# Issuing all large stores of the backward part from GpSimd, in a decode attention block with its gradients

## Chip, cores, metric

One core of one Trainium2 chip. The metric is the device time of one launch in microseconds (us), the median of several runs; lower is better.

## The reference

A pre-norm decode block, forward and backward (the vector-Jacobian product of the whole), for 4 batches and one query position. Cut to what matters:

```python
def _A_ref(x, k_cache, v_cache, wq, wo):            # B=4, H=32, Sk=4096, Dh=128, D=512
    q = (x @ wq).reshape(B, 1, H, Dh).transpose(0, 2, 1, 3)
    p = softmax(einsum("bhqd,bhkd->bhqk", q, k_cache) * Dh ** -0.5)
    o = einsum("bhqk,bhkd->bhqd", p, v_cache)
    return o.transpose(0, 2, 1, 3).reshape(B, 1, H * Dh) @ wo
h   = x + _A_ref(layernorm(x), ...)
out = h + (silu(layernorm(h) @ w1) * (layernorm(h) @ w3)) @ w2
# returned: out and the gradients of x, k_cache, v_cache, wq, wo, w1, w3, w2
```

What counts is the traffic. K and V have 128 (batch, head) pairs of 1 MB each in bf16. The forward part reads K and V once. The backward part reads V again and writes two gradients of the same size, gk (of the K cache) and gv (of the V cache): 128 x 3 MB, and some 20 MB of weights and weight gradients. Each gk and gv is an outer product of a column and a row, so they are cheap to make and dear to write.

## The kernel before

All big tiles live in 22 slots of 8 KB per partition, handed out from a queue: what is given back goes to its end, what is taken comes from its front. The rotation is fixed when the program is built; a slot whose last user is a store is waited for until that store has landed.

```python
free = deque(range(NSLOT))                 # NSLOT = 22
class Slot:
    def __init__(self, name):
        self.i = free.popleft()
        self.t = slotp.tile([P, SLOT], BF16, name=name, tag=f"slot{self.i}")
    ...
    def give(self):
        free.append(self.i)
```

The backward loop. `front` transposes V on TensorE (ScalarE copies the result out) and makes dP; `back` makes gv and gk on VectorE and stores them. GpSimd copies a column of P ahead of each gv. Loads of V run up to 7 heads ahead.

```python
def load_V2():
    ...
    nc.sync.dma_start(out=V2s[s].heads(), in_=cache_head(A_v_cache, s))        # L749
def front(s):
    ...                                                     # transposes of V, dP on TensorE
    nc.gpsimd.tensor_copy(out=P2[:], in_=P_all[:, s, :, None].to_broadcast([P, SJ, 2]))
def back(s):
    gv = Slot("gv")
    outer(gv.heads(), P2, reps["rdo", s // REP][:, s % REP, :])                # VectorE
    nc.gpsimd.dma_start(out=rows_of(out_3[b, h]), in_=gv.heads())              # L1065
    gv.give()
    ...                                                     # dS from dP, c, P
    gk = Slot("gk")
    outer(gk.heads(), dS2, reps["rq", s // REP][:, s % REP, :])                # VectorE
    nc.sync.dma_start(out=rows_of(out_2[b, h]), in_=gk.heads())                # L1075
    gk.give()
for s in range(NH):
    prefetch(s + 1)                                         # load_V2 while slots allow
    if s + 1 < NH: front(s + 1)
    back(s)
    step("s", 1 if s < 42 else 2 + s % 2)                   # a piece of the weight gradients
```

The weight gradients (gwq, gw of w2, w1 and w3, gwo) are made beside this by `side_work`, in 14 tiles, for example:

```python
for h0 in range(0, H, 8):
    st = Slot("gwo")
    for k in range(8):
        h = h0 + k
        grad_unit(st.b(8 * D)[:, k * D:(k + 1) * D], oflat.b(HD)[0:B, h * P:(h + 1) * P], dh_bf[0:B, :])
        yield
    nc.sync.dma_start(out=out_5[h0 * P:(h0 + 8) * P, :].rearrange("(h p) j -> p h j", p=P), ...)   # 1 KB rows in HBM
    st.give()
```

## Time and profile before

| | before |
|---|---|
| median, 3 runs | 1774.19 us (1772.02 to 1779.35) |
| profiled run | 1788.03 us, 0.8% above that median |
| backward part | 735 us to the end, DMA share 0.99, 396 GB/s |
| DMA queues there | q1 (SyncE) 278.63 MB, q0 (GpSimd) 134.23 MB |

In the slices of a page every digit is a tenth of busy time. A DMA issue line tells who issued, how often, how large, and the median time from issue to landing. From the page of the kernel before:

```profile
V<-in_A_v_cache_dram SPq DMA_DIRECT2D x128, 1024.0 KB, 23.2
out_dram<-gv POOLq DMA_DIRECT2D x128, 1024.0 KB, 11.2
out_dram<-gk SPq DMA_DIRECT2D x128, 1024.0 KB, 21.3
```

Three transfers of the same size; the one that has GpSimd's queue almost to itself lands in half the time. The prediction shows the other views.

### The profile page before, as it was taken

To read this page: it belongs to the slowest core of one execution; us is meant where nothing else is said; L and a number is where in the kernel's file an instruction comes from. 1 tells how busy PE (TensorE), PEld (TensorE's weight loads), DVE (VectorE), ACT (ScalarE), POOL (GpSimd) and SP (SyncE) were. 2 spreads that over 40 slices of the span, in tenths; PEclk is the share of its full clock that TensorE was granted. 3 is DMA by queue.
4 is the path that set the end of the run, shared out by engine and by line. 5 is a ranking of instruction groups with operands and counts; after the bars stand their busy time and mean duration, and the time that the engine had idled before them with its cause. 6 is when DMAs were issued, how large, how long until landed. Compare 5 with 4: busy or idle time off the path is not lost.

```text
span 1786.1 us, 43979 instructions
## 1 busy us (share of the span) xinstructions
PE 1315.1 (74%) x18993; PEld 1110.2 (62%) x18993; DVE 1254.9 (70%) x1385; ACT 954.8 (53%) x1460; POOL 488.2 (27%) x663
## 2 busy tenths in 40 slices
PE   5888888788888888888588845776778575664753
PEld 4677666666676666877487744564566454554653
DVE  5899899899989984577466835466465557464674
ACT  3455544445445445555365635575577565564743
POOL 2333333333333320231112313123222123132331
PEclk8999999999999999655555556665565556555655
DMA  9999999999999996999999999999999999999998
GB/s 399 410 418 417 420 418 419 419 415 418 413 401 412 404 414 206 373 419 411 390 396 414 401 362 418 400 349 422 405 404 386 407 407 392 365 357 382 414 416 357
DMA packets 112050, 707.85 MB, mean 396 GB/s; under 512 B 11232, under 2 KB 24808, under 8 KB 28912
## 3 DMA queue, kind: packets, MB, share of 16 engines
q1 hardware_dynamic: 93360, 570.80, 79.0%
q0 software_dynamic: 18496, 134.24, 18.5%
q8 instruction: 149, 2.44, 0.5%
q14 instruction: 45, 0.37, 0.1%
HBM read 422.58 MB, written 282.34 MB: 395 GB/s over the span
## 4 chain that ended last, share of the span: by engine, by line
DMA 40%; DVE 10%; PE 6%; ACT 4%; issue 3%; SPq 1%; POOL 0%; DVEq 0%; ACTq 0%
DMA out_dram<-gk 30%; DVE gv L1053 5%; DVE gk L1053 3%; ACT VT L740 3%; DMA out_dram<-gw 3%; DMA out_dram<-gwq 2%; DMA out_dram<-gv 2%; PE pt_tps L739 2%; DMA dqflat<-dqr_bf 1%; SPq L749 1%; DMA V<-in_A_v_cache_dram 1%; DMA w<-in_B_w_dram 1%; DVE PK L421 1%; DVE dS L1071 0%; PE M_ps L436 0%
## 5 line engine op out<-in xcount | busy, mean ns | idle before, releaser
L740 ACT COPY VT<-pt_tps 128x1024 bf16<-128x1024 bf16 x512 | 492.1, 1016 | 270.5 <-PE pt_tps L739 146.2
L739 PE MATMUL pt_tps<-ident_b,V 128*128 128x128 bf16 x4096 | 450.6, 292 | 169.5 <-ACT VT L740 169.4
L739 PEld LDWEIGHTS <-V 128*128 128x128 bf16 x4096 | 400.2, 137 | 235.0 <-issue 219.1
L1053 DVE TENSOR_TENSOR gv<-P,reps 128x4096 bf16<-128x4096 bf16 x128 | 294.5, 2301 | 210.7 <-DMA out_dram<-gk 164.7
L1053 DVE TENSOR_TENSOR gk<-dS,reps 128x4096 bf16<-128x4096 bf16 x128 | 294.1, 2298 | 96.4 <-DMA out_dram<-gk 74.5
L421 DVE TENSOR_TENSOR PK<-Kn,PK 128x4096 bf16<-128x4096 bf16 x128 | 302.9, 2366 | 37.6 <-POOL PK L417 37.6
L436 PE MATMUL M_ps<-PK,Vn 128*128 128x130 bf16 x4096 | 284.9, 222 | 56.6 <-DMA Vn<-in_A_v_cache_dram 56.3
L436 PEld LDWEIGHTS <-Vn 128*128 128x128 bf16 x4096 | 251.5, 99 | 77.6 <-DMA Vn<-in_A_v_cache_dram 71.0
L1065 POOL DMA_DIRECT2D out_dram<-gv x128 | 68.3, 534 | 774.4 <-DVE dSt L1068 675.3
L328 DVE STREAM_TRANSPOSE KT<-Kn 128x512 f32<-128x512 f32 (+1 forms) x321 | 250.9, 798 | 0.5 <-issue 0.5
L323 ACT COPY KT<-pt_tps 128x1024 bf16<-128x1024 bf16 x128 | 129.5, 1013 | 192.9 <-PE pt_tps L322 157.1
L1046 PE MATMUL dP_ps<-dOT_bf,VT 128*128 128x1 bf16 x4096 | 149.2, 166 | 95.4 <-ACT VT L740 58.4
L1046 PEld LDWEIGHTS <-VT 128*128 128x128 bf16 x4096 | 140.3, 104 | 107.7 <-ACT VT L740 68.5
L1049 POOL COPY P<-P_all 128x64 bf16<-128x64 bf16 x128 | 196.6, 1537 | 0.0
L336 POOL COPY zq<-qT_bf 128x2 bf16<-128x2 bf16 x128 | 152.3, 1190 | 0.0
L417 POOL COPY PK<-P_all 128x64 bf16<-128x64 bf16 x128 | 32.6, 254 | 437.5 <-ACT P_all L411 432.2
L411 ACT COPY P_all<-pt_P 32x64 bf16<-32x64 bf16 x256 | 52.3, 204 | 59.4 <-PE pt_P L407 57.2
L322 PE MATMUL pt_tps<-ident_b,Kn 128*128 128x128 bf16 x1024 | 79.6, 222 | 0.7 <-DVE qrep L282 0.7
L446 PE MATMUL kP_ps<-PK,onesw 128*32 128x512 bf16 x1024 | 79.6, 388 | 0.0
L322 PEld LDWEIGHTS <-Kn 128*128 128x128 bf16 x1024 | 61.3, 99 | 26.5 <-issue 26.5
L400 ACT ACTIVATE Pn<-E,rl 128x1024 bf16<-128x1024 f32 x64 | 73.8, 1153 | 2.8 <-DVE rl L397 2.8
L354 PE MATMUL S_ps<-KT,W 128*32 128x256 bf16 x1536 | 74.7, 285 | 0.0
(216 smaller groups left out, 1204.8 us busy)
## 6 DMA issues: line engine op xcount, KB each, us to landing
Kn<-in_A_k_cache_dram SPq DMA_DIRECT2D x128, 1024.0 KB, 14.8
Vn<-in_A_v_cache_dram SPq DMA_DIRECT2D x128, 1024.0 KB, 15.4
V<-in_A_v_cache_dram SPq DMA_DIRECT2D x128, 1024.0 KB, 23.2
out_dram<-gv POOLq DMA_DIRECT2D x128, 1024.0 KB, 11.2
out_dram<-gk SPq DMA_DIRECT2D x128, 1024.0 KB, 21.3
wq<-in_A_wq_dram SPq DMA_DIRECT2D x8, 1024.0 KB, 15.3
out_dram<-gw SPq DMA_DIRECT2D x6, 896.0 KB, 23.6
wo<-in_A_wo_dram SPq DMA_DIRECT2D x4, 1024.0 KB, 13.6
```

The costliest lines, as they stand in the source:

```text
L322: nc.tensor.transpose(pt[:, i, :], Kn[:, c * GW + i, :], ident_b[:])
L323: nc.scalar.copy(out=KT[:, c * GW:(c + 1) * GW, :], in_=pt[:])
L328: nc.vector.transpose(out=KT[:, c * w_:(c + n) * w_], in_=Kn[:, c * w_:(c + n) * w_])
L336: nc.gpsimd.tensor_copy(out=zq[gi % 2][hl][:, 32:132:67], in_=qT_bf[:, s:s + 1].to_broadcast([P, 2]))
L421: nc.vector.tensor_tensor(out=PK[:, :, 0:Dh].rearrange("p j (r t) -> p j r t", t=2), in0=Ks[s].heads().rearrange("p j (r t) -> p j r t", t=2),
L436: nc.tensor.matmul(hold["M"][:], lhsT=Vn[:, j, :], rhs=PK[:, j, :], start=(j == 0), stop=(j == SJ - 1))
L446: nc.tensor.matmul(hold["kP"][32 * q:32 * (q + 1), :, :], lhsT=ones_window(w), rhs=PK[:, j0:j0 + 4, 0:Dh], start=(w == 0 and c == 0), stop ...
L739: nc.tensor.transpose(pt[:, i, :], Vn[:, g * GW + i, :], ident_b[:])
L740: nc.scalar.copy(out=VT[:, g * GW:(g + 1) * GW, :], in_=pt[:])
L1046: nc.tensor.matmul(dP_ps[:, j:j + 1], lhsT=VT[:, j, :], rhs=dOT_bf[:, s:s + 1], start=True, stop=True)
L1049: nc.gpsimd.tensor_copy(out=P2[:], in_=P_all[:, s, :, None].to_broadcast([P, SJ, 2]))
L1053: nc.vector.tensor_tensor(out=dst.rearrange("p j (r t) -> p j r t", t=2), in0=col2[:, :, None, :].to_broadcast([P, SJ, Dh // 2, 2]), in1=r ...
```

## The change

Intent: SyncE's in-order queue holds loads and stores, and each can stand in front of the other. All stores of the backward part but two tiny ones go to GpSimd, which issues gv already, so that SyncE has the loads (and four small copies for each of two flattenings).

```diff
-                nc.sync.dma_start(out=out_4[cc * P:(cc + 1) * P, :], in_=st.b(HD))
+                nc.gpsimd.dma_start(out=out_4[cc * P:(cc + 1) * P, :], in_=st.b(HD))
 ... (the same word for out_8, for out_6 and out_7, and for out_5)
-            nc.sync.dma_start(out=rows_of(out_2[b, h]), in_=gk.heads())
+            nc.gpsimd.dma_start(out=rows_of(out_2[b, h]), in_=gk.heads())
```

More of the change, by code (lines that the diff above doesn't have):

```diff
@@ L982, in side_work @@
                     yield
-                nc.sync.dma_start(out=out_8[i * 7 * P:(i + 1) * 7 * P, :].rearrange("(c p) j -> p c j", p=P),
+                nc.gpsimd.dma_start(out=out_8[i * 7 * P:(i + 1) * 7 * P, :].rearrange("(c p) j -> p c j", p=P),
                                   in_=st.b(7 * D).rearrange("p (c j) -> p c j", c=7))
@@ L993, in side_work @@
                             yield
-                    nc.sync.dma_start(out=out_ap[i * 2 * P:(i + 1) * 2 * P, :].rearrange("(c p) f -> p c f", p=P),
+                    nc.gpsimd.dma_start(out=out_ap[i * 2 * P:(i + 1) * 2 * P, :].rearrange("(c p) f -> p c f", p=P),
                                       in_=st.b(2 * F).rearrange("p (c f) -> p c f", c=2))
@@ L1012, in side_work @@
                     yield
-                nc.sync.dma_start(out=out_5[h0 * P:(h0 + 8) * P, :].rearrange("(h p) j -> p h j", p=P),
+                nc.gpsimd.dma_start(out=out_5[h0 * P:(h0 + 8) * P, :].rearrange("(h p) j -> p h j", p=P),
                                   in_=st.b(8 * D).rearrange("p (h j) -> p h j", h=8))
```

## The prediction

> **What bounds the kernel now.** I read the page's slices first, then the windows, then the DMA queues, then the waits, because a change of issuing engine can only pay where an issue is late. The slices give the load on the 16 DMA engines and the rate:
>
> ```profile
> DMA  9999999999999996999999999999999999999998
> GB/s 399 410 418 417 420 418 419 419 415 418 413 401 412 404 414 206 373 419 411 390 396 414 401 362 418 400 349 422 405 404 386 407 407 392 365 357 382 414 416 357
> ```
>
> One slice is 44.7 us. Slices 17 to 40 are the backward part (735 us to the end); slice 16 is the middle part between the two. The DMA row is full in both parts, but the rate is 418 or so in most of the forward part and moves between 349 and 422 in the backward part. So the backward part is bound by bytes, with some loss. The windows say how much (columns: stretch, length, busy time of PE, PEld, DVE, ACT, POOL with counts, PE clock, DMA share, GB/s):
>
> ```profile
> 40.00:640.00 600.00, 503.00 (x8455) 414.25 (x8453) 543.50 (x725) 297.05 (x663) 204.18 (x354) 0.99 1.01 414
> 1500.00:1650.00 150.00, 91.95 (x1130) 75.05 (x1128) 80.92 (x65) 83.82 (x104) 38.85 (x33) 0.56 0.96 371
> 1650.00:1760.00 110.00, 74.29 (x1074) 67.97 (x1073) 77.46 (x64) 67.51 (x74) 35.51 (x31) 0.61 1.01 416
> 735.00:1780.00 1045.00, 713.07 (x8889) 612.94 (x8887) 635.75 (x523) 598.83 (x700) 263.01 (x253) 0.58 0.99 396
> ```
>
> No engine is near its bound in 1045 us (PE 713, DVE 636, ACT 599, POOL 263); the DMA engines are, at 0.99. The last 110 us, where side work is over and only V loads and gv and gk stores run, reach 416 GB/s; the 150 us before, with the gwo stores, only 371. The queues in that whole window, 735 to 1780 (packets, MB, share of the 16 engines):
>
> ```profile
> DMA packets 66018, 414.17 MB, mean 396 GB/s; under 512 B 6702, under 2 KB 14390, under 8 KB 17462
> q1 hardware_dynamic: 47496, 278.63, 66.7%
> q0 software_dynamic: 18431, 134.23, 31.6%
> ```
>
> q1 is what SyncE issues (V loads, gk stores, all weight gradients), q0 what GpSimd issues (gv stores). Per MB they cost the same engine time: 66.7/278.63 = 0.239% and 31.6/134.23 = 0.235%. Where a store is issued makes its bytes no cheaper. Next, who waits on SyncE in the window (total us, times, longest):
>
> ```profile
> SPq L1075 <- DVE gk L1053: 520.2, 98, 16.2
> ```
>
> and on VectorE:
>
> ```profile
> DVE gv L1053 <- DMA out_dram<-gk: 164.7, 37, 23.6
> DVE gk L1053 <- DMA out_dram<-gk: 74.5, 18, 13.9
> ...
> DVE gv L1053 <- DMA out_dram<-gv: 4.7, 4, 1.4
> ```
>
> SyncE spends 520 us standing at a gk store whose data VectorE has not made; V loads behind it cannot go. VectorE waits 239 us for the slots of gk stores and almost never (4.7 us here, 2.7 at gk's line) for those of gv: the page's issue list has gk landing after 21.3 us, gv after 11.2. The reverse blocking is in SyncE's timeline (start, duration):
>
> ```profile
> 1577.18 0.51 SPq L1013 DMA_DIRECT2D out_dram<-gwo  x1
> 1579.59 14.85 SPq L749 DMA_DIRECT2D V<-in_A_v_cache_dram  x1
> 1594.54 1.84 SPq L1075 DMA_DIRECT2D out_dram<-gk  x1
> ```
>
> An issue that usually takes 0.33 us takes 14.85 us: the ring is full, behind a gwo store cut into 1 KB rows. The gk store behind it is held, VectorE runs out of slots, and afterwards the DMA engines run short (share 0.81 in 1590 to 1600).
>
> **What the Trainium skill says.** (1) "DMA: Bandwidth & Descriptors", section "Issuing engines are not separate DMA queues": DMAs from all three issuers share the same 16 engines and interleave, and spreading them only saves issue time. The trace agrees: 0.239 against 0.235% per MB. (2) Same page, "Queues, rings and completion order": each DMA engine takes turns between the rows that have work, a packet at a time. The trace agrees in that gv, nearly alone on q0, lands in 11.2 us while gk, sharing q1 with the loads, needs 21.3; in 1020 to 1030, q0 had 50.9% and q1 49.3% of the engine time. (3) "SBUF — State Buffer", in the part on the three doors: GpSimd and VectorE share a port pair under an exclusive lock, and descriptors of GpSimd's DMAs cannot be written while VectorE holds it. The trace agrees for GpSimd's own copies: a 128x64 copy of P took 0.25 us at 1546.96 with VectorE idle, and 2.03 to 2.3 us beside a gk or gv product, mean 1537 ns. For descriptors the trace shows only that the issue itself always took 533 ns; when they were written is not visible.
>
> **The change part by part.** It moves 142 stores from SyncE to GpSimd: 128 gk, 4 gwq, 6 gw, 4 gwo. The instruction order shows nothing else: SyncE 555 rows to 413, GpSimd 668 to 810, TensorE, VectorE and ScalarE the same. Buffers are the same 22 slots in the same rotation; only the semaphores of the slot waits change.
>
> - Removed: the coupling of loads and stores in one in-order queue. The visible loss is DMA idle time. I took 10 us windows with a share well below 1: 1060 (0.73), 1150 (0.86), 1180 (0.52), 1530 (0.72), 1560 (0.92), 1590 (0.81), 1630 (0.83). Their shortfalls add up to 0.27+0.14+0.48+0.28+0.08+0.19+0.17 = 1.61 windows, 16 us. Four follow a gwo store as above; 1060 and 1180 fall where SyncE stands at small copies of the dq chain (20.3 us on the critical chain for dqflat) and at the small output of L945 (10.8 us), which stay on SyncE, but with no gk store behind them any more. I choose 60% of this as recovered: minus 10 us.
> - Moved: gk and gv in one ring, in the order in which VectorE needs their slots back. Their landing times should meet between 11.2 and 21.3, about 16 us. VectorE's 239 us of waits shrink or spread, but beside DMA engines that are full that is worth nothing by itself. Some windows are full and slow (374 GB/s in 870 to 880, 367 in 1040 to 1050, compute all waiting); a smoother mix may win a little: minus 5 us, a guess.
> - Added: 142 issues x 0.533 us = 76 us on GpSimd, which is busy 263 of 1045 us; per head one copy (1.54) and two issues (1.07) make 2.6 us of the 1045/128 = 8.2 us that a head takes. Not a bound.
> - Added: each gk store becomes ready just as VectorE starts the next gv product. If its descriptors wait for the port, it starts up to 2.3 us later. 128 x 2.3 = 294 us of latency, nearly all behind a filled ring; I charge 1%: plus 3 us.
>
> Sum: -10 - 5 + 3 = -12 us: 1774 - 12 = 1762 us. The forward part does not change.
>
> **The rivals.** (a) The transfers are hidden anyway: the DMA is full, bytes and their cost are the same, and nothing moves beyond 5 us. For it: share 0.99. Time 1770 to 1776. (b) The ring takes turns better than I think, loads-only beside stores-only, and the whole backward part runs at the 416 GB/s of its last stretch: 414.17/0.416 = 996 us instead of 1045, that is 1725 us, faster by 2.8%. Against it: gw and gwo still have 1 KB and 3.5 KB rows and wq2 2 KB rows, and the window 1350 to 1380 with gw2 has 383 GB/s at full share. (c) GpSimd becomes the late issuer. All stores now share 8 completion semaphores instead of gv having 8 and gk sharing 8 with the loads, so a store waits for the eighth one before it; gwo descriptors may fill the software ring, and then gv, gk and the copies of P that VectorE needs all stand behind them. With 2.3 us more on the path in half of the heads that is 64 x 2.3 = 147 us if nothing hides it, some 1920 us; since the rings are full, I expect a tenth at most: 1775 to 1790.
>
> **Range and chances.** The repeats spread over 1772 to 1779. (a) and a small gain of my own kind are most of the weight. The range 1742 to 1786 takes in all of (a), the mild form of (c), and half of the way to (b). Faster by over 2% needs under 1739, which needs most of (b): 0.10. Slower by over 2% needs over 1810, a real stall on GpSimd: 0.06. Within 2%: 0.84.
>
> **What the changed profile would show.** q1 falls to about 279 - 128x1.05 - 14 = 130 MB in the backward part, q0 rises to about 282. The gk wait of 520 us on SyncE is gone, SyncE waits for slots instead. gv and gk land within a few us of each other. No V load issue of 12 us or longer after gwo. The windows at 1530 to 1640 and 1180 go up from 371 GB/s to about 395; the backward mean from 396 to about 401. Wrong if: GpSimd's issues grow far beyond 0.53 us, VectorE waits for POOL's P copy (0.2 us now), the cost per MB of q0 rises above 0.24%, or the backward mean reaches 410 and more, which would mean that the in-order coupling costs rate and not only idle time.

## The result

| | before | changed |
|---|---|---|
| median, 4 runs each | 1776.77 us (1772.02 to 1780.30) | 1754.76 us (1749.15 to 1756.07) |
| ratio | | 0.9872, interval 0.9837 to 0.9907 |

A ratio is the mean time of one kernel's runs over the mean of the other's of the same rounds, so it is not quite the ratio of the medians. The kernel is faster by 1.3%, some 22 us, and its outputs are correct. The two profiled runs lie further apart, 1786.1 and 1747.4 us of span, since before was profiled in a run longer than all its timed ones and the changed kernel in its shortest; differences between these two profiles below are therefore too large, 38.7 us of span against the 22 us of the medians.

The slices after:

```profile
DMA  9999999999999998699999999999999999999997
GB/s 398 410 418 418 419 418 419 418 412 418 418 415 398 418 407 313 257 422 421 410 414 418 415 416 413 422 383 426 417 418 416 414 412 406 422 407 410 424 417 303
```

The forward part is as it was. In the backward part the dips to between 349 and 365 are gone but for one of 383 and the last slice, where only a rest of stores is left. The windows (columns as in the prediction):

```profile
1500.00:1650.00 150.00, 90.82 (x1192) 77.64 (x1191) 87.42 (x70) 83.59 (x100) 35.48 (x56) 0.57 1.01 415
735.00:1740.00 1005.00, 720.34 (x8888) 621.02 (x8885) 634.79 (x523) 598.66 (x700) 262.75 (x395) 0.57 1.00 412
```

Nearly the same busy time of every engine as before, in windows of 1005 and 1045 us. The queues, 735 to 1742 us:

```profile
DMA packets 61129, 414.43 MB, mean 412 GB/s; under 512 B 6710, under 2 KB 8510, under 8 KB 12542
q0 software_dynamic: 39578, 282.31, 68.0%
q1 hardware_dynamic: 21459, 130.79, 31.6%
```

The bytes are where they should be. The packets under 2 KB fell from 14390 to 8510: that is the 1 KB rows of 4 gwo (1024 each) and 2 gw stores (896 each), 5888 in all, within 8 of the difference. The issues on the page:

```profile
V<-in_A_v_cache_dram SPq DMA_DIRECT2D x128, 1024.0 KB, 11.1
out_dram<-gv POOLq DMA_DIRECT2D x128, 1024.0 KB, 19.6
out_dram<-gk POOLq DMA_DIRECT2D x128, 1024.0 KB, 19.6
```

gv and gk now land alike; the loads have become the quick ones. What VectorE waits for (us in total, times, longest), and SyncE's V load issues (duration min/median/max in ns):

```profile
DVE gv L1053 <- DMA out_dram<-gk: 141.1, 41, 8.6
DVE gv L1053 <- DMA out_dram<-gv: 40.5, 16, 6.9
...
DVE gv L1053 <- POOL P L1049: 2.5, 2, 1.4
```

```profile
L749 SPq DMA_DIRECT2D V<-in_A_v_cache_dram x128: 327/328/6808, 695.0 to 1663.7; - x128
```

Before, one wait for gk reached 23.6 us and one V load issue 23.3 us; now the longest are 8.6 and 6.8. The sum hardly moved: for slots of gk and gv stores together VectorE waited 247 us before and 234 now, spread over both. GpSimd does not become late: VectorE waits 2.5 us for its copies in all.

**One number for the experiments.** To separate idle DMA engines from dear bytes I use two figures of each run, over the window from 735 us to 10 us before the end: the share of the 16 DMA engines that q0, q1 (and q10, ScalarE's ring) took, and that share times the window over their MB. Before, 735 to 1776 us:

```profile
q1 hardware_dynamic: 47399, 277.96, 66.9%
q0 software_dynamic: 18377, 133.85, 31.6%
```

That is 66.9% + 31.6% = 98.5% of 1041 us for 411.81 MB, 2.490 us per MB. Changed, 735 to 1737 us:

```profile
q0 software_dynamic: 39540, 282.04, 68.3%
q1 hardware_dynamic: 21459, 130.79, 31.8%
```

That is 100.1% of 1002 us for 412.83 MB, 2.430. The changed kernel's second profile gave 2.422, so differences under 0.01 mean little. (The shares are sums of packet durations and can pass 100%.)

Both figures come from one profiled execution, while the ratios below come from all. The profiled execution lay above the median of its kernel by 11 us in before, 8 in swap, 7 in gk_only and 5 in side_only, and within 3 us in the others of the table (6 below in the first profile of the change), and nothing tells whether the extra was idle time or dear bytes. Even if all of it is taken off the cost per MB, before, swap and side_only stay at 2.46 to 2.47. A share that differs by 1%, some 10 us, between two profiles is not safe in the same way.

### The profile page after: what moved, and what is told of

It is laid out like the page before. It is cut to its first block, busy times and chain, and to the rows that moved or that the text cites. A ratio compares the mean times of both kernels' runs of the same rounds, so it can differ in the third digit from the quotient of the medians.

```text
span 1747.4 us, 44078 instructions
## 1 busy us (share of the span) xinstructions
PE 1324.0 (76%) x18993; PEld 1120.0 (64%) x18993; DVE 1254.4 (72%) x1385; ACT 953.7 (55%) x1460; POOL 487.4 (28%) x805
## 2 busy tenths in 40 slices
DMA packets 107123, 707.86 MB, mean 405 GB/s; under 512 B 11232, under 2 KB 18920, under 8 KB 23984
## 4 chain that ended last, share of the span: by engine, by line
DMA 38%; DVE 11%; issue 6%; PE 4%; ACT 3%; POOL 1%; DVEq 0%; POOLq 0%; ACTq 0%; SPq 0%
DMA out_dram<-gk 22%; DMA out_dram<-gv 12%; DVE gk L1053 4%; DVE gv L1053 4%; DMA V<-in_A_v_cache_dram 2%; ACT VT L740 2%; PE pt_tps L739 1%; DMA out_dram<-gw 1%; POOL P L1049 1%; DMA w<-in_B_w_dram 1%; DVE PK L421 1%; DVE dS L1071 0%; PE M_ps L436 0%; DVE dSt L1068 0%; PE o_ps L961 0%
## 5 line engine op out<-in xcount | busy, mean ns | idle before, releaser
L739 PE MATMUL pt_tps<-ident_b,V 128*128 128x128 bf16 x4096 | 458.2, 296 | 147.0 <-ACT VT L740 147.0
L739 PEld LDWEIGHTS <-V 128*128 128x128 bf16 x4096 | 408.1, 140 | 211.6 <-issue 202.1
L1075 POOL DMA_DIRECT2D out_dram<-gk x128 | 68.2, 533 | 384.3 <-DVE gk L1053 377.1
L1049 POOL COPY P<-P_all 128x64 bf16<-128x64 bf16 x128 | 117.4, 918 | 0.0
## 6 DMA issues: line engine op xcount, KB each, us to landing
V<-in_A_v_cache_dram SPq DMA_DIRECT2D x128, 1024.0 KB, 11.1
out_dram<-gv POOLq DMA_DIRECT2D x128, 1024.0 KB, 19.6
out_dram<-gk POOLq DMA_DIRECT2D x128, 1024.0 KB, 19.6
out_dram<-gw POOLq DMA_DIRECT2D x6, 896.0 KB, 21.7
```

The costliest lines, as they stand in the source:

```text
L739: nc.tensor.transpose(pt[:, i, :], Vn[:, g * GW + i, :], ident_b[:])
```

## The experiments

Twelve kernels, each beside its own runs of the kernel before. All gave correct outputs. The share, the us per MB and the landing times (medians) are of each kernel's one profile, in the window just named.

| run | gk | gv | weight gradients | V loads | ratio | interval | share | us per MB | gk / gv / V land, us |
|---|---|---|---|---|---|---|---|---|---|
| before | SyncE | GpSimd | SyncE | SyncE | 1 | | 98.5% | 2.490 | 21.3 / 11.3 / 23.9 |
| after_same | GpSimd | GpSimd | GpSimd | SyncE | 0.9873 | 0.9848 to 0.9897 | 99.7% | 2.422 | 19.5 / 19.2 / 11.1 |
| gk_only | GpSimd | GpSimd | SyncE | SyncE | 0.9939 | 0.9915 to 0.9963 | 98.5% | 2.445 | 18.8 / 18.7 / 22.7 |
| side_only | SyncE | GpSimd | GpSimd | SyncE | 0.9956 | 0.9931 to 0.9981 | 99.6% | 2.476 | 22.2 / 11.3 / 25.6 |
| swap | GpSimd | SyncE | SyncE | SyncE | 0.9998 | 0.9967 to 1.003 | 99.3% | 2.493 | 11.2 / 23.6 / 24.7 |
| gk_act | ScalarE | GpSimd | SyncE | SyncE | 0.9976 | 0.9958 to 0.9993 | 98.2% | 2.437 | 13.9 / 14.1 / 26.8 |
| mirror | SyncE | SyncE | SyncE | GpSimd | 0.9854 | 0.9835 to 0.9873 | 100.4% | 2.439 | 18.8 / 19.0 / 11.7 |
| before_contig | SyncE | GpSimd | SyncE, long rows | SyncE | 0.9947 | 0.993 to 0.9965 | 99.5% | 2.460 | 21.7 / 11.0 / 24.0 |
| after_contig_small | GpSimd | GpSimd | GpSimd, long rows | SyncE | 0.9857 | 0.9837 to 0.9876 | 99.7% | 2.429 | 19.6 / 19.3 / 11.3 |
| all_sp | SyncE | SyncE | SyncE | SyncE | 0.9864 | 0.9845 to 0.9884 | 99.7% | 2.423 | 20.0 / 19.9 / 20.0 |
| mirror_contig | SyncE | SyncE | SyncE, long rows | GpSimd | 0.9849 | 0.9829 to 0.9868 | 100.2% | 2.424 | 19.8 / 19.5 / 11.7 |
| after_pact | GpSimd | GpSimd | GpSimd | SyncE | 0.9899 | 0.9873 to 0.9925 | 99.9% | 2.429 | 19.5 / 19.0 / 11.4 |
| gk_act_late | ScalarE, one head late | GpSimd | GpSimd | SyncE | 0.9845 | 0.9826 to 0.9864 | 99.4% | 2.427 | 12.8 / 19.8 / 22.7 |

Several expectations speak of the mean duration of a packet of 8 KB. In the same windows the traces give 323.4 ns in before, 317.5 in gk_only, 315.8 in gk_act, 316.8 in mirror, 315.1 in all_sp and 315.6 in gk_act_late.

### First call: which part of the change does it

**after_same**, the changed kernel unaltered, is the yardstick.

> The changed kernel again, unaltered, as the yardstick of this call. Both theories: about 0.987 of the kernel before (0.984 to 0.991), some 1755 us; gk and gv stores land alike, near 19.6 us.

Measured 0.9873 (1752.71 us). The result repeats.

**gk_only**: the last hunk of the diff alone.

```diff
-            nc.sync.dma_start(out=rows_of(out_2[b, h]), in_=gk.heads())
+            nc.gpsimd.dma_start(out=rows_of(out_2[b, h]), in_=gk.heads())
```

> Only the 128 gk stores go to GpSimd; the 14 weight-gradient stores stay on SyncE. Theory 1 (the loss before was that loads and gk stores hold each other up in one in-order queue): nearly the whole gain, 0.988 to 0.991, and the full-rate packets of 8 KB get shorter as in the changed kernel. Theory 2 (the loss was the weight-gradient stores, cut into 1 KB packets that fill the hardware ring): little, 0.995 to 1.000, with V load issues of over 12 us after gwo still there.

**side_only**: the other four hunks, gk stays.

```diff
-                nc.sync.dma_start(out=out_5[h0 * P:(h0 + 8) * P, :]...
+                nc.gpsimd.dma_start(out=out_5[h0 * P:(h0 + 8) * P, :]...
 ... (and out_4, out_6, out_7, out_8)
```

> Only the 14 weight-gradient stores (gwq, gw, gwo) go to GpSimd; gk stays on SyncE with the loads. Theory 1: 0.996 to 1.000. Theory 2: 0.988 to 0.992; no packets near 1 KB any more from those stores, no V load issue of over 12 us, the 1500 to 1650 us stretch rises from 371 to about 410 GB/s.

Neither theory had it alone: 0.9939 and 0.9956, whose product 0.9895 is within the interval of the whole change. The two figures suggest that the halves work in different ways. Moving gk leaves the share at 98.5% and lowers the cost of a MB from 2.490 to 2.445 us; moving the weight gradients leaves the cost nearly (2.476) and raises the share to 99.6%. SyncE's V load issues tell the second half, here in gk_only, where the weight gradients stayed with the loads, in the window from 735 us:

```profile
L749 SPq DMA_DIRECT2D V<-in_A_v_cache_dram x118: 327/328/28192, 740.5 to 1682.4; - x118
```

and in side_only:

```profile
L749 SPq DMA_DIRECT2D V<-in_A_v_cache_dram x119: 327/1105/5429, 742.2 to 1706.0; - x119
```

With the gwo stores in the loads' ring, the V load issue behind the third of them takes 28 us; without them none takes over 5.4 us.

**swap** exchanges the roles of gk and gv.

```diff
-            nc.gpsimd.dma_start(out=rows_of(out_3[b, h]), in_=gv.heads())
+            nc.sync.dma_start(out=rows_of(out_3[b, h]), in_=gv.heads())
-            nc.sync.dma_start(out=rows_of(out_2[b, h]), in_=gk.heads())
+            nc.gpsimd.dma_start(out=rows_of(out_2[b, h]), in_=gk.heads())
```

> gk goes to GpSimd and gv comes back to SyncE, the weight-gradient stores stay: the same split of bytes between the queues as before, with the roles exchanged. Theory 1 (any store stream in the queue of the loads costs): 0.998 to 1.003, and VectorE now waits for gv instead of gk. Theory 3 (it is gk, the last in the slot order, that must be off the load queue): as gk_only, 0.988 to 0.992.

0.9998 and 2.493 us per MB: it is not a matter of gk. The page's issues show the mirror of before: whichever store shares the loads' queue is slow:

```profile
V<-in_A_v_cache_dram SPq DMA_DIRECT2D x128, 1024.0 KB, 23.8
out_dram<-gv SPq DMA_DIRECT2D x128, 1024.0 KB, 23.5
out_dram<-gk POOLq DMA_DIRECT2D x128, 1024.0 KB, 11.2
```

Theory 3 is out. I took this for a proof of theory 1, too early, as the third call shows. This run also speaks against the short rows as a cause by themselves. They stand in the loads' ring here too, and the V loads behind the four gwo stores take 11.8 to 18.1 us to issue, yet the share is 99.3% and no 10 us window from 1500 to 1640 us falls below 0.95 (before has four there):

```profile
L749 SPq DMA_DIRECT2D V<-in_A_v_cache_dram x119: 327/600/18132, 739.7 to 1715.0; - x119
```

### Second call: the rings, and the short rows

**gk_act** gives gk a second hardware ring, ScalarE's.

```diff
-            nc.sync.dma_start(out=rows_of(out_2[b, h]), in_=gk.heads())
+            nc.scalar.dma_start(out=rows_of(out_2[b, h]), in_=gk.heads())
```

> gk stores from ScalarE's queue, a second hardware ring without loads; gv on GpSimd, weight-gradient stores on SyncE. Theory 4 (what makes a MB cheaper is that stores and loads are not in one ring, whoever writes the descriptors): packets of 8 KB of gk and gv at about 315 to 318 ns as with gk on GpSimd (before: 321 to 324), engine time per MB about 2.445 us instead of 2.490, time 0.990 to 0.998 (ScalarE stands in order at gk, which may cost some of it). Theory 5 (it is the software ring): packets stay at 321 to 326 ns, time 0.998 to 1.01.

The bytes became cheap (2.437), so software descriptors are not the reason. The time is only 0.9976. The share, 98.2%, is the lowest of all, though by the two figures alone the gain would be about that of gk_only, so they do not account for the time. I put it down to ScalarE standing in order at gk's data before its copies for the next head; gk_act_late, below, tests that. The trace shows that this was not all: in the window ScalarE waits 72.5 us for gk products and 106 us for V loads to land, and before shows neither wait.

**mirror** sends the loads through GpSimd and all stores through SyncE, with P's copy on ScalarE.

```diff
-            nc.sync.dma_start(out=V2s[s].heads(), in_=cache_head(A_v_cache, s))
+            nc.gpsimd.dma_start(out=V2s[s].heads(), in_=cache_head(A_v_cache, s))
-            nc.gpsimd.dma_start(out=rows_of(out_3[b, h]), in_=gv.heads())
+            nc.sync.dma_start(out=rows_of(out_3[b, h]), in_=gv.heads())
-            nc.gpsimd.tensor_copy(out=P2[:], in_=P_all[:, s, :, None].to_broadcast([P, SJ, 2]))
+            nc.scalar.copy(out=P2[:], in_=P_all[:, s, :, None].to_broadcast([P, SJ, 2]))
```

> The mirror image: the V loads of the backward part go to GpSimd, all stores stay on or go to SyncE; the small copy of P moves to ScalarE so that GpSimd can stand at a load without holding it. Loads and stores are apart again, but stores are now on the hardware ring. Theory 4: packets of 8 KB at about 316 ns on both queues and a time of 0.985 to 0.995, a little worse than the changed kernel since the 1 KB packets remain. Theory 5: packets of the stores at 321 ns and more, 0.997 to 1.01.

0.9854: as good as the change. Which generator writes the stores' descriptors makes no difference that these runs can see, and the 1 KB rows do no harm in a ring whose jam holds up no load. Here are its queues, from 735 us to 10 us before the end; the hardware ring now has the stores:

```profile
q1 hardware_dynamic: 48783, 288.04, 69.9%
q0 software_dynamic: 17136, 124.79, 30.5%
```

**before_contig** leaves every issue where it was, and gives each partition neighbouring rows of the output, so that a row in HBM is 7 or 8 KB long.

```diff
-   grad_unit(st.b(8 * D)[:, k * D:(k + 1) * D], oflat.b(HD)[0:B, h * P:(h + 1) * P], dh_bf[0:B, :])
+   grad_unit(st.b(8 * D)[:, k * D:(k + 1) * D], oflat.b(HD)[0:B, h0 * P + k:(h0 + 8) * P:8], dh_bf[0:B, :])
-   out_5[h0 * P:(h0 + 8) * P, :].rearrange("(h p) j -> p h j", p=P)
+   out_5[h0 * P:(h0 + 8) * P, :].rearrange("(p h) j -> p h j", p=P)
 ... (the same for out_8 with 7 rows and for out_6, out_7 with 2)
```

> The kernel before, all issues as they were, but the three weight-gradient stores with short rows are laid out so that a partition holds 7 or 8 neighbouring rows of the output (rows of 7 to 8 KB in HBM instead of 1 and 3.5 KB); same bytes, same products. If the gain of moving the weight-gradient stores alone (0.9956) was the hardware ring filling with short packets: the same here, 0.993 to 0.998, and no V load issue over 8 us. If it was their place in SyncE's order: 0.998 to 1.002.

0.9947, the same gain as side_only without moving anything, and the share is again up, 99.5%. The longest V load issue falls to 5.3 us:

```profile
L749 SPq DMA_DIRECT2D V<-in_A_v_cache_dram x119: 327/961/5284, 742.6 to 1702.0; - x119
```

So in this arrangement the second half of the change's gain can be had by moving the short rows or by making them long. How it comes about is less sure: the cost per MB is lower as well (2.460), and swap has the same jams without the idle time.

**after_contig_small** adds the long rows and moves the two small outputs in the changed kernel.

```diff
-            nc.sync.dma_start(out=o1_2, in_=dx_bf)
+            nc.gpsimd.dma_start(out=o1_2, in_=dx_bf)
 ... (o0_2 likewise, and the long rows of before_contig)
```

> The changed kernel with those long rows too, and with the two small outputs (the 4x512 stores) issued from GpSimd, so that SyncE does not stand 32 and 14 us at them with V loads behind. Packets cost some 2 us less; the one window with a low DMA share (0.73 at 1160 us) fills: minus 3 us. Expected 0.982 to 0.987, against 0.987 of the changed kernel, so hardly outside its interval.

0.9857: no difference from the change that the intervals allow one to claim. With the share at 99.7% there is nothing left to unblock.

### Third call: the cause doubled, and two controls

By now my theory 4 was that a ring in which loads and stores are mixed makes bytes dearer. **all_sp** puts everything in one ring.

```diff
-            nc.gpsimd.dma_start(out=rows_of(out_3[b, h]), in_=gv.heads())
+            nc.sync.dma_start(out=rows_of(out_3[b, h]), in_=gv.heads())
```

> The suspected cause doubled: gv comes back to SyncE, so that the V loads and all stores of the backward part go through one hardware ring. Theory 4 (loads and stores mixed in one ring make a MB dearer): packets of 8 KB at 328 ns or more against 321 to 324 before, engine time per MB 2.50 to 2.55 us, time 1.003 to 1.02. If sharing a ring only costs by late issues, packets stay at 324 ns or less and only idle time grows.

A clear miss: 0.9864, 2.423 us per MB, as good as the change. One line of difference from the kernel before, in the opposite direction of the change, and the same gain. The page's issues:

```profile
V<-in_A_v_cache_dram SPq DMA_DIRECT2D x128, 1024.0 KB, 20.0
out_dram<-gv SPq DMA_DIRECT2D x128, 1024.0 KB, 19.9
out_dram<-gk SPq DMA_DIRECT2D x128, 1024.0 KB, 20.0
```

and VectorE's waits from 735 to 1737 us, which have not become fewer but shorter (at most 11.0 us against 23.6 before):

```profile
DVE gv L1053 <- DMA out_dram<-gk: 172.3, 50, 11.0
DVE gv L1053 <- DMA out_dram<-gv: 57.8, 20, 5.4
DVE gk L1053 <- DMA out_dram<-gv: 44.2, 16, 5.0
```

So mixing loads and stores in a ring does not make them dear, and an order in which a store stands behind a load does not cost by itself. Theories 1 and 4 both fall as I had put them. Even the jam behind gwo is still there (V load issues of 10.36, 6.08, 11.94 and 10.29 us behind the four gwo stores) and costs nothing visible.

**mirror_contig** and **after_pact** are controls: the mirror image with long rows, and the changed kernel with only P's copy on ScalarE (edits shown above).

> The mirror image (loads on GpSimd, stores on SyncE) with the long rows for the weight-gradient stores. Rows of 1 KB cost 428 us of 16 engines' time in all, long ones some 390, so 2 us; stalls of the ring no longer hold loads in any case: 0.982 to 0.986, within noise of the mirror image's 0.9854.

0.9849 (1747.39 us), within the mirror image's interval. It has the lowest median; against the changed kernel, 1752.71 and 1754.76 us, the intervals of the ratios overlap, so only its lead over before is shown.

> The changed kernel with only the copy of P moved to ScalarE, as in the mirror image, to see whether that move and not the exchange of queues made the mirror image's 0.9854. If the copy is off the path, as VectorE's 2.5 us of waits for it say: 0.985 to 0.989, no different from the changed kernel's 0.987.

0.9899, if anything a little worse, within the intervals. VectorE now waits 69.8 us for the copies of P on ScalarE. The copy is not what made the mirror image fast.

### Fourth call: must gk and gv share a ring?

In after, mirror and all_sp, gk and gv share a ring; in before, swap, side_only and before_contig they do not, and bytes are dear. gk_act, with the two apart and 2.437, already spoke against a need to share, but its time had not followed. **gk_act_late** separates them without a jam: everything as in the change, but gk in ScalarE's ring and issued one head late.

```diff
+        late = deque()
+        def flush_gk():
+            if late:
+                b_, h_, sl = late.popleft()
+                nc.scalar.dma_start(out=rows_of(out_2[b_, h_]), in_=sl.heads())
+                sl.give()
         def back(s):
             b, h = bh_of(s)
+            flush_gk()
 ...
-            nc.gpsimd.dma_start(out=rows_of(out_2[b, h]), in_=gk.heads())
-            gk.give()
+            late.append((b, h, gk))
 ... (and one flush_gk() after the loop)
```

> gv and the weight-gradient stores from GpSimd as in the changed kernel, but gk from ScalarE's hardware ring, one head late so that ScalarE does not stand at it; loads alone on SyncE. So gk is off the load ring, and not in gv's ring. It compares with the changed kernel (gk in gv's ring, 0.987) and the weight-gradient stores moved alone (gk in the load ring, 0.9956). Theory 6a (gk and gv have to be in one ring): 0.993 to 0.998. Theory 6b (it is enough that gk and gv land equally fast, whatever the rings): both land within 2 us of each other, packets of 8 KB below 318 ns, 0.985 to 0.990.

0.9845, so they need not share a ring (6a falls). Nor need they land alike: 12.8 and 19.8 us, a gap of 7 us, is a miss for 6b's number too, at 2.427 us per MB:

```profile
out_dram<-gv POOLq DMA_DIRECT2D x128, 1024.0 KB, 19.8
out_dram<-gk ACTq DMA_DIRECT2D x128, 1024.0 KB, 12.8
```

Against gk_act it also shows that the late issue, with the weight gradients moved as well, brings the share from 98.2% back to 99.4% and ScalarE's waits from 72.5 to 28 us for gk products and from 106 to 52 us for V loads; which of the two did more is not separated.

### What stands after twelve runs

Shown: in all four arrangements with dear bytes (before, swap, side_only, before_contig: 2.460 to 2.493 us per MB) exactly one of the two big stores is in the loads' ring and the other has another ring. In all nine others (2.422 to 2.445) both are in the loads' ring or neither is. The nearest two, 2.460 and 2.445, are only 0.6% apart, but the times say the same: to bring the odd store to the other, one edit alone, made 0.9939 (gk_only), 0.9864 (all_sp) and, from side_only to the change, 0.9873/0.9956 = 0.992, and to exchange the two (swap) nothing; only gk_act's time hardly followed. Shown as well: to move the weight gradients' short rows out of the loads' ring, or to make them long, is worth some 0.5% of the whole time in the arrangement of before. It went with less idle time of the DMA engines (share 98.5% in before and gk_only, 99.5% or more without the rows), but swap (99.3%) and all_sp (99.7%) keep the rows there without the idle time. That the jam causes it is therefore argued, not shown.

Argued only: if two rings take turns, a ring with two thirds of the bytes gets half of the turns while the other has work, so gv runs ahead and gk and the loads fall behind, and a jam in the slow ring empties half as fast. The landing times fit this (11 beside 22 to 24 us), and so do the jams (12.8 to 23.3 us in before, 6.1 to 11.9 in all_sp). When both stores are in the crowded ring, the ring that falls behind is either paced evenly with all (all_sp) or faces a quick ring with the loads alone, which are 7 heads ahead (the change). But in gk_act_late the shares are about a third each and no ring is crowded, so it says only that this too is harmless.

Open: why the same bytes take 0.6 to 2.9% more engine time in the bad arrangement. It is neither the generator of the descriptors (mirror, gk_act), nor the mixing of directions in a ring (all_sp), nor the short rows (before_contig, 2.460, still dearer). The packets in the traces narrow it down. The median packet of 8 KB takes 309 ns in every run; what differs is how many take over 400 ns: 4.3, 4.2, 3.9 and 3.4% in before, swap, side_only and before_contig, and 1.5 to 2.2% in the nine others. The time above 309 ns, divided by 16 engines, is 43.5 us in before and 21.2 in the first profile of the change, nearly the whole difference in cost (0.060 x 412 = 25 us). So not every byte is dearer: a few packets are held up. What holds them up, no run here tests.

## Why the prediction was right or wrong

The time, 1754.76 us, lies in the range of 1742 to 1786 and within 2%; the gain of 22 us was nearly twice the 12 that I had summed. The range allowed any gain up to 32 us, and about half of the gain came by a way that I had ruled out, so that the time fell inside is partly luck. By its steps:

- **Bound by bytes, no engine near its bound.** Right. Busy times are the same after, in less time.
- **"Where a store is issued makes its bytes no cheaper."** This is the step that failed. I compared q0 with q1 within one run (0.235 and 0.239% per MB) and concluded that the arrangement was indifferent. Both queues were dear together. Across runs the same bytes cost 2.490 and 2.430 us per MB. One line of mine that would show it wrong was a backward mean of 410 GB/s and more; it came out at 412, in the changed kernel's fastest run. The reason I had attached to that line, in-order coupling of loads and stores, is refuted by all_sp. The other line, q0 above 0.24% per MB, was badly put: q0 came to 0.241%, but of a shorter window.
- **Idle time, minus 10 us.** About right in size: side_only gives (1 - 0.9956) x 1777 = 8 us (3 to 12 by its interval), and of the 10 us windows with a low share one is left in the changed kernel (1160, 0.73). The cause that I read from the timeline, gwo's rows filling the ring, fits before_contig, whose V loads behind gwo issue in at most 1.7 us, but in swap and all_sp the same jams left no such idle time.
- **A smoother mix, minus 5 us, called a guess.** The mis-sized term: gk_only gives (1 - 0.9939) x 1777 = 11 us (7 to 15), at an unchanged DMA share. Mechanism unexplained, as above.
- **The port lock, plus 3 us.** Nothing of it shows: all_sp has no software DMA in the backward part, and the changed kernel has 282 MB of them; 0.9864 and 0.9873. But each interval is 0.2% wide to either side, 3.5 us, so a cost of 3 us is not excluded. I had also stretched the page. "SBUF — State Buffer" says of VectorE's two-port modes that they keep GpSimd from writing descriptors, and in "Who interferes with whom" it reports that products of two tensors, which gv and gk are (TENSOR_TENSOR in the profile), did not stall DMAs.
- **GpSimd's 142 more issues, 76 us, not a bound.** Right: gk's issue has a median of 532 ns, gwo's took 0.91 us, and VectorE waited 2.5 us for GpSimd.
- **Landing times.** They met, as said, but at 19.6 us and not at 16.
- **The rivals.** (a), hidden anyway, is wrong: the DMA share of 0.99 hid that the cost per byte could fall. (b), the whole stretch at its best rate of 416 GB/s, came near in the rate of that one run, 412, for a reason I had not named, but 22 us is less than half of its 49. (c), a late GpSimd, did not happen.

## What to carry to other kernels

A DMA share of 0.99 does not mean that only bytes are left to cut: compare the engine time per MB across arrangements, not across the queues of one run. If several large streams feed one loop, try the plain arrangements (all in one queue; loads apart from stores) before one that splits two equal stores over a crowded and an empty queue. Stores with short rows in a queue in which loads stand are worth a test, moved or with long rows: here that gave 0.5% in the arrangement of before.

## What the Trainium skill lacked or had wrong

- "DMA: Bandwidth & Descriptors", "Issuing engines are not separate DMA queues", says that issuing from several engines only saves issue time. One queue alone is indeed as good as two (all_sp 0.9864, the change 0.9873), but spreading can also cost: with gk in the loads' queue and gv in another, the kernel took 1.4% longer than with all in one queue (before against all_sp, one line apart), at 2.49 against 2.42 us of engine time per MB. The page has no such case.
- The same page, in "SWDGE vs HWDGE vs iDMA", gives for a packet of the software path preferably at most 4096 B. The trace agrees for rows of 1 KB: packets under 2 KB fell by 5888 on the page of the whole run (24808 to 18920) when these rows moved to GpSimd, and 1472 packets of 4096 B came in their place. Rows of 8 KB went as packets of 8192 B on both paths, above that size. That the hardware path of this chip sends each row of 1 KB as a packet of its own is not said there, and these counts show it.
- No page says how soon a hardware ring fills. Behind one gwo store of 1024 rows of 1 KB, the next V load's issue took 2 to 28 us instead of 0.33 (the sixteen cases of before, gk_only, swap and all_sp); behind one with rows of 8 KB, 0.3 to 1.7 us (before_contig).
